# Where four tiles' statistics stand in VectorE's queue: an FNet and MLP layer on one Trainium2 core

## The chip, the core and the metric

The kernel runs on one core of a Trainium2 chip. Five engines work side by side, each through its own queue in order: TensorE (PE, matrix products into PSUM), VectorE (DVE), ScalarE (ACT), GpSimd (POOL) and SyncE (SP, which issues the DMAs). They wait for each other through semaphores. The metric is the device time of one execution in microseconds (us), smaller is better.

## The reference, cut to what matters

```python
xn = _layernorm(x, axis=-1)                       # x: (1, 2048, 576), no weights
# A: FNet mixing, the real part of a 2-D Fourier transform by matrices
a = einsum("bsd,ed->bse", xn, dft_hid_re); b = einsum("bsd,ed->bse", xn, dft_hid_im)
y = einsum("ts,bse->bte", dft_seq_re, a) - einsum("ts,bse->bte", dft_seq_im, b)
# B: MLP, 576 -> 4608 -> 576
h = maximum(einsum("bsd,df->bsf", xn, w1), 0)
out = x + y + einsum("bsf,fd->bsd", h, w2)
```

Every row of x (a token) is normalised by its own mean and variance before anything else can use it.

## The kernel before, in words

The 2048 rows are 16 tiles of 128 (tiles 0 to 15), in four groups of four. The hidden width of 4608 is cut into nine blocks of 512. All operands of products are split into two float16 parts, high and low, so each product is three matmuls; the second MLP product and the sequence transform use seven products in place of eight (Strassen in Winograd's form, `PRODUCTS`, L263).

A tile's way to TensorE has these steps. `stats` (L175) takes, for a list of tiles, two `bn_stats` of each (L182, VectorE), an aggregate of each (L185), one square root for all (L192, ScalarE), and six short VectorE steps (L193 to L204) that give the factors and shifts. `normalize` (L219) writes the normalised rows in float32 on VectorE (L224) and in float16 on ScalarE (L225). `remainder` (L227) takes the low parts, for most tiles on GpSimd (L229, L232). `transposes` (L236) turns nine pieces on TensorE (L240) into a PSUM tile `pt` and copies them to `xT` on ScalarE (L245, L248). A staging buffer of pool `dpool` (four buffers) carries a tile from `normalize` to `transposes`.

The MLP then runs over steps (block b, group g). `mlp1` (L291) makes one 128 x 512 piece of the hidden layer in 14 matmuls (L286); a block has four pieces. `mlp1_out` (L296) takes two pieces, a pair, out of PSUM: ReLU and splitting (L303, L306 and L313 on ScalarE; L307 to L311 on VectorE) and a last VectorE difference (L314), which is remembered as `order["lo"]`. `mlp2` (L318) is one of the seven second products, 12 matmuls (L328), and an accumulation into the rows on VectorE (L334). Step n computes the first product of its own group and the second product of the step before it, interleaved.

Ahead of that loop the first block's first two groups are written out by hand: `tile_by` makes the first product tile by tile in pieces of 128 columns, `max_w1`, `power_w1` and `split_w1` scale and split w1, and `prepare_w2` (L426) does so for w2: sums on ScalarE (L375), a power of two found with two small matmuls (L140, L148), and splits on ScalarE (L164) and VectorE (L165, with L405 to L408 between them). Of group 1's first product only the first pair (two pieces, in a PSUM tile `pq` of pool `ps2`) is made by hand; the other two pieces are made at step n = 1. `ps2` has two buffers, which `pq`, the `pt` tiles and the second products share.

While b is 0, each step also prepares the next group: at n = 1 tiles 8 to 11, at n = 2 tiles 12 to 15. That is the call `weave(stats(...))` at L627 and, between the pieces, `normalize`, `remainder` and `transposes` (L636 to L638).

The order of each engine's queue isn't the order of the source. The framework records all instructions with their dependencies and places them by its own costs. `tc.issue_after(ins)` adds one rule: the instructions recorded inside it, on the engine of `ins`, stand behind `ins` in that queue. It adds no semaphore. At n = 1, `order["lo"]` is the difference L314 of group 1's first pair; at n = 2, that of its second pair.

After the MLP come the hidden transform (`dft1`, L678) and the sequence transform (L779), which take no part in the change.

Of the kernel before, what the change touches and what calls it, by code (L numbers as in the profile page):

```python
# [41 lines left out]
def kernel(  # L42
# [127 lines left out]
    means, factors, shifts, order = {}, {}, {}, {}  # L170
# [4 lines left out]
    def stats(ts):  # L175

        n = len(ts)
        mv = small.tile([P, n, 2], F32, tag=f"mv{n}", name=f"mv{ts[0]}")
        sts = [small.tile([P, 2, 6], F32, tag="st", name=f"st{t}", bufs=4) for t in ts]
        for t, st in zip(ts, sts):  # L180
            for j in range(2):
                nc.vector.bn_stats(st[:, j, :], acc[t][:, j * EH : (j + 1) * EH])  # L182
                yield
        for i, st in enumerate(sts):
            nc.vector.bn_aggr(mv[:, i], st.rearrange("p a b -> p (a b)"))  # L185
            yield
        r0, u, r, sh = (
            small.tile([P, n], F32, tag=f"{a}{n}", name=f"{a}_{ts[0]}") for a in ("r0", "u", "r", "sh")
        )
        m, v = mv[:, :, 0], mv[:, :, 1]  # L190
        stt = nc.vector.scalar_tensor_tensor
        nc.scalar.activation(u, v, AF.Sqrt, bias=eps)  # L192
        nc.vector.reciprocal(r0, u)  # L193
        yield

        stt(u, v, EPS, r0, ALU.add, ALU.mult)
        yield
        nc.vector.tensor_tensor(u, u, r0, ALU.mult)
        yield
        nc.vector.tensor_scalar(u, u, -0.5 * SX, 1.5 * SX, ALU.mult, ALU.add)  # L200
        yield
        nc.vector.tensor_tensor(r, u, r0, ALU.mult)
        yield
        stt(sh, m, -1.0, r, ALU.mult, ALU.mult)  # L204
        for i, t in enumerate(ts):
            means[t], factors[t], shifts[t] = mv[:, i, 0:1], r[:, i : i + 1], sh[:, i : i + 1]

    def weave(steps, *others):

        others = list(others)  # L210
        for _ in steps:
            if others:
                others.pop(0)()
        for f in others:
            f()
# [3 lines left out]
    def normalize(t, eng=nc.vector):  # L219
        stage = dpool.tile([P, 5 * EH], F32, tag="d", name=f"xn{t}")  # L220
        xn = xns[t] = stage[:, :D]

        xs = xss[t] = stage[:, D : 2 * D].bitcast(F16)
        eng.tensor_scalar(xn, acc[t], means[t], factors[t], ALU.subtract, ALU.mult)  # L224
        nc.scalar.activation(xs[:, :D], acc[t], AF.Identity, bias=shifts[t], scale=factors[t])  # L225

    def remainder(t, eng):  # L227
        xn, xs = xns[t], xss[t]
        eng.tensor_tensor(  # L229
            xs[:, D : D + REM], xn[:, KM * P :], xs[:, KM * P : D], ALU.subtract  # L230
        )
        eng.tensor_tensor(  # L232
            xs[:, D + REM :], xn[:, : KM * P], xs[:, : KM * P], ALU.subtract
        )

    def transposes(t):  # L236
        xs = xss[t]
        pt = ps2.tile([P, 2, 1024], F16, tag="ps2", name=f"pt{t}")
        for k in range(NKX):
            nc.tensor.transpose(  # L240
                pt[:, k // 8, (k % 8) * P : (k % 8 + 1) * P], xs[:, k * P : (k + 1) * P], ident
            )
        g, c = divmod(t, TG)
        dst = xT[g][:, :, c * P : (c + 1) * P]
        nc.scalar.activation(  # L245
            dst[:, :8, :], pt[:, 0, :].rearrange("p (k t) -> p k t", t=P), AF.Copy
        )
        nc.scalar.activation(dst[:, 8, :], pt[:, 1, :P], AF.Copy)  # L248
# [42 lines left out]
    def mlp1(b, g, i):  # L291
        ps = ps1.tile([P, G], F32, tag="ps1", name=f"p1_{b}_{g}_{i}")
        mlp1_group(b, g, i, slice(0, G), ps)
        return ps

    def mlp1_out(b, g, i, pa, pb):  # L296

        h = hs[b, g, i] = mlp.tile([P, 2, 7, GH], F16, tag="h", name=f"h{b}_{g}_{i}", bufs=4)
        st = mlp.tile([P, 5, GH], F32, tag="stage", name=f"s{b}_{g}_{i}")
        stt = nc.vector.scalar_tensor_tensor  # L300
        a11, a21, a12, a22 = pa[:, :GH], pa[:, GH:], pb[:, :GH], pb[:, GH:]
        r21, s1, s2, s3, s4 = (st[:, n] for n in range(5))
        nc.scalar.activation(r21, a21, AF.Relu)  # L303
        for q, src in ((slice(A11, A11 + 1), a11), (slice(A12, A22 + 1), pb)):
            hi, lo = (h[:, n, q].rearrange("p a b -> p (a b)") for n in range(2))
            nc.scalar.activation(hi, src, AF.Relu)  # L306
            stt(lo, src, 0.0, hi, ALU.max, ALU.subtract)  # L307
        stt(s3, a11, 0.0, r21, ALU.max, ALU.subtract)
        stt(s1, a22, 0.0, r21, ALU.max, ALU.add)
        stt(s2, a22, 0.0, s3, ALU.max, ALU.subtract)  # L310
        stt(s4, a12, 0.0, s2, ALU.max, ALU.subtract)  # L311
        hi, lo = (h[:, n, S1 : S4 + 1] for n in range(2))
        order["s"] = nc.scalar.activation(hi, st[:, 1:], AF.Copy).ins  # L313
        order["lo"] = nc.vector.tensor_tensor(lo, st[:, 1:], hi, ALU.subtract).ins  # L314
# [121 lines left out]
    def prepare_block(b):  # L436

        wait = [lambda: None] * 2
        (m0, s0), (m1, s1) = prepare_w1(b, 0), prepare_w1(b, 1)
        return (  # L440
            [lambda: (load_w1(b, 0), load_w1(b, 1))] + wait
            + m0 + m1 + s0 + [lambda: load_w2(b, 0)] + s1 + [lambda: load_w2(b, 1)]
            + wait + prepare_w2(b)
        )
# [96 lines left out]
    def work():  # L541
        if todo:
            todo.pop(0)()
# [5 lines left out]
    def load_d(j):  # L549
        load_raw(("d", j), dft[:, :, j * EH : (j + 1) * EH], [P, KT, EH])  # L550

    def power_d(j):
        if j == 0:
            sc["d"], pw["d"], mx["d"] = cell("sd", 4), cell("pd", 4), cell("md", 4)
        m = slice(j, j + 1)
        magnitude(mx["d"][:, m], raws["d", j])
        power(sc["d"][:, m], pw["d"][:, m], mx["d"][:, m])
# [5 lines left out]
    def split_d(j):  # L563
        split(dsp[j][:, 0], dsp[j][:, 1], raws["d", j], sc["d"][:, j : j + 1])
# [47 lines left out]
    for n in range(1, len(steps)):  # L612
        b, g = steps[n]
        pb, pg = steps[n - 1]
        if g == 0 and b:
            if b + 1 < NB:
                todo += prepare_block(b + 1)
            else:
                todo += [lambda: (load_d(0), load_d(1)), lambda: None, new_d, lambda: None]
                for j in range(4):  # L620
                    todo += [lambda j=j: power_d(j), lambda j=j: split_d(j)]
                    if j < 2:
                        todo += [lambda j=j: load_d(j + 2), lambda: None]
                todo += [scales_d]
        if b == 0 and g + 1 < NG:
            with tc.issue_after(order["lo"]):
                weave(stats([(g + 1) * TG + i for i in range(TG)]))  # L627
        ps = []
        for i in range(NF):
            if n > 1 or i > 1:  # L630
                ps.append(mlp1(b, g, i))
                if i % 2:
                    mlp1_out(b, g, i // 2, *ps[-2:])
            if b == 0 and g + 1 < NG:
                t = (g + 1) * TG + i
                normalize(t)  # L636
                remainder(t, nc.gpsimd)
                transposes(t)  # L638
            if n == 2 and i == 2:
                todo += prepare_block(1)  # L640
            for _ in range(1 if b else 3):
                work()
            for q in range(2 * i, min(2 * i + 2, 7)):
                mlp2(pb, pg, q)
            for _ in range(1 if b else 3):
                work()
            if n > 3 and i % 2 and passes:
                passes.pop(0)()
# [196 lines left out]
```

## Time and profile before

| what | value |
|---|---|
| median of 3 runs | 1309.46 us (1308.74 to 2731.43) |
| profiled execution | 1310.21 us |
| its span, first to last instruction | 1308.4 us |
| TensorE busy | 1273.3 us, 97% |
| VectorE busy | 973.5 us, 74% |
| ScalarE busy | 532.5 us, 41% |
| GpSimd busy | 34.6 us, 3% |
| mean granted TensorE clock | 0.991 |

How rows are read: in a timeline, the start and the length in us, engine, line, operation, tile written <- tiles read, shapes, the count of merged instructions, and in brackets the idle time ahead of them with what ended it. In the table by windows the columns are the window, its length, busy time (and instructions) of PE, PEld (weight loads), DVE, ACT and POOL, then the granted TensorE clock, the busy share of the DMA engines and GB/s. In groups by line: busy us, mean ns of one, idle us ahead and what ended it. Matmul ends are modelled, and lengths of merged rows overlap the next row a little.

### The profile page before, as it was taken

The page shows a single profiled execution, that of the slowest core. Times are in us where ns is not written, and L with a number is a line of the kernel's source. Part 1 is how long each engine was busy: PE and PEld are TensorE (multiplying, and loading weights), DVE is VectorE, ACT ScalarE, POOL GpSimd, SP SyncE. Part 2 cuts the span into 40 slices and gives each one's busy share as a digit, 9 for nine tenths or more (in the row PEclk, how much of TensorE's full clock was granted, in tenths as well). Part 3 has the DMA queues.
Part 4 walks back from the last instruction along what each step waited for, and adds up shares of the span by engine and source line. Part 5 has one row for each costly group of instructions (what it writes and reads, how often), then busy time and mean ns, then how long its engine had stood idle before and what let it go on. Part 6 is the DMA issues. An engine that isn't in the chain of part 4 may idle for free.

```text
span 1308.4 us, 21689 instructions
## 1 busy us (share of the span) xinstructions
PE 1273.3 (97%) x9080; PEld 872.4 (67%) x9080; DVE 973.5 (74%) x1671; ACT 532.5 (41%) x794; POOL 34.6 (3%) x60
## 2 busy tenths in 40 slices
PE   7589999999999999999999999999999999999998
PEld 6365666666666666666666656677777777777777
DVE  7857978577586696785875885568677887878785
ACT  5644444244253443443443432234443333343332
POOL 3030000000000000000000000000000000000000
PEclk8899999999999999999999999999999999999999
DMA  6101213123122131131221232240014344343420
GB/s 238 41 1 37 74 56 111 61 73 102 49 89 85 49 106 68 49 117 56 74 87 48 94 94 85 89 150 17 1 52 171 122 135 154 97 151 117 145 83 19
DMA packets 38002, 112.75 MB, mean 86 GB/s; under 512 B 3984, under 2 KB 10640, under 8 KB 37904
## 3 DMA queue, kind: packets, MB, share of 16 engines
q1 hardware_dynamic: 37904, 111.36, 25.7%
q8 instruction: 71, 1.16, 0.4%
q14 instruction: 27, 0.22, 0.1%
HBM read 101.91 MB, written 9.44 MB: 85 GB/s over the span
## 4 chain that ended last, share of the span: by engine, by line
PE 88%; DVE 6%; DMA 2%; ACT 2%; issue 1%; POOL 0%; SPq 0%; POOLq 0%; DVEq 0%; ACTq 0%
PE p L286 29%; PE p L328 26%; PE p L779 24%; PE pd L678 8%; DVE acc L334 1%; DVE w2s L165 1%; DMA raw_d<-in_dft_dram 1%; ACT xT L245 1%; DMA c<-in_cim_dram 1%; DVE h L307 0%; DMA acc<-in_x_dram 0%; PE pt L240 0%; DVE st L182 0%; DVE cs L165 0%; DVE c_md L98 0%
## 5 line engine op out<-in xcount | busy, mean ns | idle before, releaser
L286 PE MATMUL p<-xT,w1s 128*128 128x512 f16 (+1 forms) x2268 | 462.7, 357 | 4.0 <-ACT xT L245 3.9
L328 PE MATMUL p<-w2s,h 128*128 128x288 f16 x3024 | 396.9, 287 | 3.5 <-DVE acc L334 2.3
L328 PEld LDWEIGHTS <-h 128*128 128x128 f16 x3024 | 296.2, 98 | 105.3 <-issue 4.3
L286 PEld LDWEIGHTS <-w1s 128*128 128x128 f16 x2268 | 210.2, 99 | 206.6 <-issue 5.0
L779 PE MATMUL p<-R,cs 128*128 128x288 f16 x2688 | 329.6, 286 | 1.0 <-DVE o L785 1.0
L779 PEld LDWEIGHTS <-cs 128*128 128x128 f16 x2688 | 263.0, 98 | 67.4 <-issue 1.2
L334 DVE SCALAR_TENSOR_TENSOR acc<-p,c_ub,acc 128x576 f32<-128x576 f32 x252 | 203.4, 810 | 22.6 <-PE p L328 22.1
L164 ACT ACTIVATE cs<-c,sc_c 128x1024 f16<-128x1024 f32 x112 | 128.5, 1148 | 202.9 <-PE p L779 146.9
L307 DVE SCALAR_TENSOR_TENSOR h<-p,h 128x256 f16<-128x256 f32 (+1 forms) x144 | 79.6, 554 | 146.7 <-ACT h L306 146.6
L165 DVE SCALAR_TENSOR_TENSOR cs<-c,sc_c,cs 128x1024 f16<-128x1024 f32 x112 | 143.6, 1282 | 49.0 <-ACT cs L164 48.8
L306 ACT ACTIVATE h<-p 128x512 f16<-128x512 f32 (+1 forms) x144 | 69.7, 486 | 226.4 <-PE p L286 224.1
L313 ACT ACTIVATE h<-s 128x1024 f16<-128x1024 f32 x72 | 76.1, 1057 | 172.1 <-DVE s L311 172.0
L678 PE MATMUL pd<-dsp,xT 128*128 128x288 f16 x896 | 109.9, 286 | 0.9 <-DVE acc L334 0.9
L314 DVE TENSOR_TENSOR h<-s,h 128x1024 f16<-128x1024 f32 x72 | 87.9, 1221 | 29.0 <-ACT h L313 29.0
L678 PEld LDWEIGHTS <-xT 128*128 128x128 f16 x896 | 87.7, 98 | 23.2 <-issue 1.1
L785 DVE SCALAR_TENSOR_TENSOR o<-p,us_c,o 128x288 f32<-128x288 f32 x112 | 57.4, 513 | 20.1 <-PE p L779 20.1
L605 ACT ACTIVATE f<-f 128x1024 f32<-128x1024 f32 x64 | 66.6, 1041 | 3.6 <-DMA f<-in_cre_dram 3.6
L164 ACT ACTIVATE w2s<-raw_w,c_sw 128x576 f16<-128x576 f32 (+1 forms) x54 | 44.0, 849 | 24.6 <-DVE c_sw L397 19.7
L165 DVE SCALAR_TENSOR_TENSOR w2s<-raw_w,c_sw,w2s 128x576 f16<-128x576 f32 (+1 forms) x54 | 46.5, 910 | 7.6 <-ACT w2s L164 7.6
L303 ACT ACTIVATE s<-p 128x256 f32<-128x256 f32 x72 | 26.7, 371 | 23.5 <-PE p L286 23.5
L696 ACT ACTIVATE R<-pd,c_rho 128x288 f16<-128x288 f32 x48 | 23.9, 500 | 22.0 <-DVE T L690 12.2
L240 PE MATMUL pt<-ident,xn 128*128 128x128 f16 x144 | 12.1, 227 | 20.2 <-ACT xn L225 16.0
(96 smaller groups left out, 637.7 us busy)
## 6 DMA issues: line engine op xcount, KB each, us to landing
f<-in_cre_dram SPq DMA_DIRECT2D x32, 512.0 KB, 3.5
f<-in_cim_dram SPq DMA_DIRECT2D x32, 512.0 KB, 3.5
c<-in_cre_dram SPq DMA_DIRECT2D x32, 512.0 KB, 3.9
c<-in_cim_dram SPq DMA_DIRECT2D x32, 512.0 KB, 4.6
raw_w<-in_w_dram SPq DMA_DIRECT2D x17, 640.0 KB, 4.0
raw_w<-in_w_dram SPq DMA_DIRECT2D x18, 576.0 KB, 3.9
acc<-in_x_dram SPq DMA_DIRECT2D x16, 288.0 KB, 6.7
spill<-acc SPq DMA_DIRECT2D x16, 288.0 KB, 2.5
```

What stands on the lines that cost most here:

```text
L164: nc.scalar.activation(hi, src, AF.Copy, scale=s)
L165: nc.vector.scalar_tensor_tensor(lo, src, s, hi, ALU.mult, ALU.subtract)
L286: nc.tensor.matmul(ps[:, cols], w1s[b, i // 2][:, hl, i % 2 * KT + k], xT[g][:, kx, cols], start=(n == 0), stop=(n == len(WK) - 1),)
L306: nc.scalar.activation(hi, src, AF.Relu)
L307: stt(lo, src, 0.0, hi, ALU.max, ALU.subtract)
L313: order["s"] = nc.scalar.activation(hi, st[:, 1:], AF.Copy).ins
L314: order["lo"] = nc.vector.tensor_tensor(lo, st[:, 1:], hi, ALU.subtract).ins
L328: nc.tensor.matmul(ps[:, c], h[:, x, qa, c * P : (c + 1) * P], w[:, y, qb], start=first and i == 0 and j == 0, stop=i == NQ - 1 and j == 2 ...
L334: nc.vector.scalar_tensor_tensor(o, ps, us[b], o, ALU.mult, ALU.add)
L605: nc.scalar.activation(f, f, AF.Abs, scale=2.0**-10, accum_out=sums_c[:, n, q : q + 1])
L678: nc.tensor.matmul(ps[j], xT[g][:, kx, c * P : (c + 1) * P], dsp[j][:, hl, k], start=(n == 0), stop=(n == len(XK) - 1),)
L779: nc.tensor.matmul(ps, w[:, a, k], r[:, c, rq], start=first and k == 0 and j == 0, stop=k == HK - 1 and j == 2, skip_group_check=not first,)
```

## The change

```diff
@@ -623,7 +623,7 @@
         if b == 0 and g + 1 < NG:
-            with tc.issue_after(order["lo"]):
+            with tc.issue_after(order["lo"]) if n > 1 else nullcontext():
                 weave(stats([(g + 1) * TG + i for i in range(TG)]))
```

At n = 1 the rule is gone; at n = 2 it stays. The number of instructions, their operands and sizes are the same. What moves, in the built program:

- VectorE: the eight `bn_stats` of tiles 8 to 11 stand among the short steps of tiles 4 to 7's statistics (seven of them ahead of the normalisation of tiles 4 to 7); their aggregates, their short steps and the normalisation of tile 8 follow, ahead of the first pair's L307 of group 0. The normalisations of tiles 9, 10 and 11 stand inside the work on group 0's pairs, ahead of the w2 split. Of the seven accumulations L334 of group 0, the first now stands ahead of the last difference of group 1's first pair, and the others stand behind it and among the work on the second pair; six stand ahead of the statistics of tiles 12 to 15, the seventh among them. Before, seven of the eight `bn_stats` of tiles 12 to 15 stood ahead of all of them.
- ScalarE: the copies of tile 3 come ahead of all four normalisations of tiles 4 to 7 (before, between the second and the third). The normalisations of tiles 8, 9 and 10 stand ahead of tile 7's copies; tile 8's copies and tile 11's normalisation stand between the first and the second part of the w2 split.
- TensorE: tile 8's transposes stand straight behind tile 7's pieces of the first product (128 columns each); then 10 matmuls of the third piece of group 1, product 0 (A11 B11) of group 0, 18 matmuls of the third and fourth piece, product 1 (A12 B21), and products 2 to 6 with the transposes of tiles 9, 10 and 11 between them; then the first piece of group 2 and the transposes of tile 12. Before, the third and fourth pieces were mixed into tile 7's, tile 8's transposes came behind them, and tile 12's transposes stood ahead of group 2's first piece. Behind the transposes of tile 12 the order is the same to the end.
- GpSimd and SyncE: the same order.

## The prediction

> **What bounds the kernel now.** I read the page's engine shares and slices first, then the waits of the early stage, then the timelines of the five engines there.
>
> ```profile
> span 1308.4 us, 21689 instructions
> PE 1273.3 (97%) x9080; PEld 872.4 (67%) x9080; DVE 973.5 (74%) x1671; ACT 532.5 (41%) x794; POOL 34.6 (3%) x60
> ...
> PE   7589999999999999999999999999999999999998
> ```
>
> TensorE is busy 97% of the span, so time can come only from where it isn't: the early slices of 32.7 us (digits 7, 5 and 8). Finer windows show where the holes lie.
>
> ```profile
> 36.00:40.00 4.00, 3.44 (x58) 3.10 (x56) 2.24 (x5) 3.88 (x8) 0.00 (x0) 1.00 0.00 0
> 40.00:44.00 4.00, 2.78 (x43) 2.37 (x41) 2.90 (x14) 1.98 (x3) 0.00 (x0) 1.00 0.00 0
> ...
> 52.00:56.00 4.00, 0.00 (x0) 0.00 (x0) 4.00 (x10) 1.51 (x2) 0.00 (x0) 0.86 0.55 164
> ...
> 60.00:64.00 4.00, 0.00 (x0) 0.00 (x0) 3.86 (x19) 1.84 (x3) 0.00 (x0) 0.50 0.00 0
> ...
> 70.00:72.00 2.00, 2.00 (x11) 1.24 (x10) 1.42 (x5) 0.00 (x0) 1.14 (x2) 0.52 0.00 0
> 72.00:74.00 2.00, 2.00 (x21) 1.59 (x20) 0.95 (x3) 0.24 (x1) 0.00 (x0) 1.00 0.02 4
> ```
>
> From 52 to 64 TensorE does nothing. The granted clock holds at full through windows with holes (36 to 44), falls to 0.50 about 4 us after TensorE stops, and is back at 72. The waits between 20 and 112 us name the reason:
>
> ```profile
> PE pt L240 <- ACT xn L225: 13.4, 1, 13.4
> ```
>
> and TensorE's timeline places it:
>
> ```profile
> 26.89 0.67 PE L240 MATMUL pt<-ident,xn 128*128 128x128 f16 x9
> 27.39 3.29 PE L286 MATMUL p<-xT,w1s 128*128 128x128 f16 x56
> ...
> 36.86 0.66 PE L240 MATMUL pt<-ident,xn 128*128 128x128 f16 x9 [0.49 <-ACT xT L248]
> ...
> 43.10 7.83 PE L286 MATMUL p<-xT,w1s 128*128 128x128 f16 x56 [1.00 <-ACT xT L245]
> 64.33 0.61 PE L240 MATMUL pt<-ident,xn 128*128 128x128 f16 x4 [13.40 <-ACT xn L225]
> ...
> 67.46 6.28 PE L328 MATMUL p<-w2s,h 128*128 128x288 f16 x32
> ...
> 75.60 5.55 PE L328 MATMUL p<-w2s,h 128*128 128x288 f16 x44 [0.79 <-ACT xT L248]
> ...
> 84.80 3.18 PE L286 MATMUL p<-xT,w1s 128*128 128x512 f16 x14 [0.61 <-ACT xT L245]
> 87.82 3.10 PE L328 MATMUL p<-w2s,h 128*128 128x288 f16 x24
> 90.76 3.18 PE L286 MATMUL p<-xT,w1s 128*128 128x512 f16 x14
> ```
>
> At 64.33 the transposes of tile 8 start after 13.40 us idle: tile 8 had no normalised rows, since its statistics stand behind a VectorE difference. From 84.80 on TensorE hardly waits.
>
> **A ledger.** Both programs issue the same TensorE work between two marks: the start of tile 7's first product (43.10; the row of x56 holds it and two 128x512 groups) and the first 24 matmuls of group 1's second product (87.82). At full clock: 128x512 costs (87.82-84.80)/14 = 0.216 us, 128x288 (90.76-87.82)/24 = 0.1225. So 7.83 for the x56, 5 transposed tiles at 0.5 (26.89 to 27.39), 84 matmuls of 0.1225 = 10.3, the last group 3.02: 23.65 us. Before takes 44.72. The 21.1 between them is idle time and the half clock (the 32 matmuls at 67.46 took 6.2 instead of 3.9), and is the most that this stage can give.
>
> **The change, step by step.** In the built program all of it lies ahead of 90 us; past the transposes of tile 12 TensorE's order is unchanged, GpSimd's and SyncE's are unchanged throughout, and no DMA is added or moved.
>
> ```profile
> 23.32 0.41 DVE L185 BATCH_NORM_AGGREGATE mv<-st 128x2 f32<-128x12 f32 x4
> ...
> 26.16 2.09 DVE L224 TENSOR_SCALAR xn<-acc,mv,r 128x576 f32<-128x576 f32 x4
> 32.99 0.42 DVE L307 SCALAR_TENSOR_TENSOR h<-p,h 128x256 f16<-128x256 f32 x1 [4.75 <-ACT h L306]
> ...
> 45.17 2.14 DVE L165 SCALAR_TENSOR_TENSOR w2s<-raw_w,c_sw,w2s 128x864 f16<-128x864 f32 x2
> ...
> 54.62 0.81 DVE L165 SCALAR_TENSOR_TENSOR w2s<-raw_w,c_sw,w2s 128x576 f16<-128x576 f32 x1
> ...
> 57.41 2.97 DVE L182 BATCH_NORM_STATS2 st<-acc 128x6 f32<-128x288 f32 x8
> ...
> 99.41 1.53 DVE L98 TENSOR_REDUCE c_mf<-raw_w 128x1 f32<-128x640 f32 x2
> ```
>
> *Statistics.* Eight at 0.37 (2.97/8), four aggregates at 0.1, six short steps at 0.2: some 4.6 us, out of 57.41 to 62.9 and into the slots from 23.7 on, where VectorE sat idle 4.75 us ahead of 32.99. Seven stand ahead of the normalisation of tiles 4 to 7, but partly in the gaps of its chain: I make that start 26.74, +0.6. x has landed by then:
>
> ```profile
> L80 SPq DMA_DIRECT2D acc<-in_x_dram x16: 392/432/838, 0.7 to 16.1; - x16
> ...
> DMA to landing us min/median/max: 2.9/6.7/8.0
> ```
>
> The last of 16 loads is issued at 16.1 and the slowest takes 8.0; tile 11 is four issues of 0.43 earlier, so at most 22.4, ahead of 23.7.
>
> *ScalarE.* All four normalisations of tiles 4 to 7 now stand behind tile 3's copy, and three of tiles 8 to 10 ahead of tile 7's.
>
> ```profile
> 26.60 1.62 ACT L225 ACTIVATE xn<-acc,sh,r 128x576 f16<-128x576 f32 x2
> ...
> 31.22 1.02 ACT L245 ACTIVATE xT<-pt 128x1024 f16<-128x1024 f16 x1 [0.40 <-PE pt L240]
> ...
> 36.50 0.32 ACT L248 ACTIVATE xT<-pt 128x128 f16<-128x128 f16 x1
> ...
> 42.02 1.02 ACT L245 ACTIVATE xT<-pt 128x1024 f16<-128x1024 f16 x1 [2.15 <-PE pt L240]
> ```
>
> Tile 3's transposes end at 27.55, its copies at 28.8; four normalisations at 0.76 (half of 1.62 less the overlap) end at 31.8, the square root of tiles 8 to 11, taken as a third of one, at 32.05, and tile 4's copy starts there instead of at 31.22: +0.83, which was on the chain. Nothing after it up to tile 5's copy (ending 36.82, then 37.65) gives that back, so tile 6's transposes start at 37.7 instead of 36.86. The three extra normalisations (2.4 us) fall into the 2.15 idle ahead of 42.02; tile 7's copy starts at 42.85. Tile 7's product starts at **43.9, +0.8**; the w2 split goes from 45.17 to 46.15 on VectorE, +1.0. In it VectorE is never idle, so its last split ends at 56.4 (before 55.43) and the last read of the pair's PSUM tile (L311) at 55.7, one split of 0.72 ahead of that.
>
> *TensorE after 43.9.* 28 matmuls to 45.45; tile 8's transposes to 45.95 (ScalarE's rows for them are done at 41.4, GpSimd's remainders by 44.1 even at the worst price below, 2.7); 10 of the third group's matmuls to 48.1. Product 0 needs a PSUM slot from tile 8's copy, which stands on ScalarE behind the w2 split (to 46.8) and two short reads: 48.6, **idle 0.5**. It ends at 50.1, the 18 remaining 128x512 at 54.0. Product 1 needs the PSUM slot read by L311: 55.75, **idle 1.7**; it ends at 57.2. From there each product waits for VectorE's accumulation of an earlier one (about 0.75 us each, and L314, L307 to L311 between them):
>
> ```profile
> L334 DVE SCALAR_TENSOR_TENSOR acc<-p,c_ub,acc 128x576 f32<-128x576 f32 x8 | 6.5, 816 | 4.5 <-PE p L328 4.5
> ...
> L314 DVE TENSOR_TENSOR h<-s,h 128x1024 f16<-128x1024 f32 x4 | 4.9, 1220 | 2.5 <-ACT h L313 2.5
> ```
>
> Accumulations 0, 1, 2 end at 57.1, 59.0, 59.75 (L314, 1.15, between the first two). Product 2 runs 57.2 to 58.7; tile 9 waits for accumulation 1 (**0.35**), 9 matmuls for accumulation 2 (**0.25**) to 60.9; product 3 and 3 matmuls to 62.75; product 5 waits for accumulation 3 (63.2, **0.5**) to 64.7; 10 matmuls to 65.9, tile 10 to 66.45, 2 matmuls to 66.7; tile 11 waits for tile 10's copy (67.7, **1.05**) to 68.25; the next group waits for tile 11's (69.35, **1.2**) and runs 69.4 to 72.45.
>
> *What is late next.* Tile 12. Its statistics still follow the difference L314 and here accumulation 5 (65.85): 8 statistics and accumulation 6 to 69.6, aggregates 70.0, square root and chain 71.5, ScalarE's normalisation 72.45, then GpSimd:
>
> ```profile
> 64.35 1.31 POOL L229 TENSOR_TENSOR xn<-xn 128x64 f16<-128x64 f32 x1 [30.93 <-ACT xn L225]
> 65.63 1.37 POOL L232 TENSOR_TENSOR xn<-xn 128x512 f16<-128x512 f32 x1
> ...
> 68.34 0.30 POOL L229 TENSOR_TENSOR xn<-xn 128x64 f16<-128x64 f32 x1
> 68.60 1.15 POOL L232 TENSOR_TENSOR xn<-xn 128x512 f16<-128x512 f32 x1
> ```
>
> 1.45 for the two remainders without contention (68.34, 68.60), 2.7 at worst (64.35, 65.63): 73.9 to 75.15, and 0.25 of transposes. VectorE works through tiles 13 to 15 beside it, as it worked beside the two slow rows, so I take 75.1, near the slow end: **idle 2.1**. The Trainium skill, "GPSIMD Engine Reference", section "8. Key points", says that GpSimd shares its SBUF interfaces with VectorE, in contention with some of its instructions; the 1.31 against 0.30 us for the same 64-column step agrees; by that rule the mark would lie at the slow end, 75.4.
>
> **Sum.** The second mark: 43.9 + 23.65 + 7.65 idle = 75.2, against 87.82: **12.6 us earlier**. From there the order is the old one and TensorE never waits long, so the gain stays to the end. The profiled execution took 1310.21 (span 1308.4 and 1.8 around it): **1297.6 us**, a span of 1295.8. The median of the runs shown, 1309.46, is 0.75 lower, which I leave in the range. About 2%, 26 us, is what a measurement of this kernel tells from no change; 12.6 is under it.
>
> **Rivals.**
> *A. VectorE takes over as the bound (chance 0.20).* The wait for tile 8 is replaced by the accumulation chain: three products wait on VectorE, and every copy on ScalarE is followed by another wait of 0.8 to 1.2. My hand-overs are 0.05 us each; some forty in series, and a chain of late copies, could cost 3 to 7 more. For: VectorE is busy 4.00 of 4 in 52 to 56 and 3.86 in 60 to 64. Against: the same chain at 67 to 84 shows stops of only 0.79 and 0.61. Time 1300.5 to 1304.5.
> *B. Fewer stalls (0.10).* Tile 12's wait and half of the others vanish: gain 15 to 18, 1292 to 1295.5. The bound is 21.1.
> *C. The clock doesn't hold (0.05), the slower side.* Before, TensorE rests once for long, then runs on; after, it stops about eight times between 48 and 74. If the clock stood at 0.50 all that stretch, as at 60 to 72, its 23 us of work would take 23 longer, up to 5 of it inside waits: the mark at 93 to 98, 5 to 10 us slower, 1315.5 to 1320.5. It ends slower once over 12.6 us of work run at half clock net of waits. Against: windows with 0.56 and 1.22 us of holes kept 1.00, and my longest is 1.7 where the fall took 4. The Trainium skill, "TensorE: Matmul & The Clock Gate", section "A second HAM failure mode: psum-queue depth-cycling", describes this: short stops between groups of matmuls make the gate swing between half and full clock. No row of this trace shows it; by it the time would lie anywhere between 1297.6 and the end of this rival.
> *D. Given back later, or no effect (0.08).* The next block's w1 loads come no earlier, since they wait for the w2 split:
>
> ```profile
> 52.08 3.71 SPq L90 DMA_DIRECT2D raw_w<-in_w_dram  x2
> ```
>
> Issued at about 53 and 56.5, read first at about 87 (99.41 before): they would have to be 25 us late. An unmoved order would give 1310, but the built order has the statistics ahead of 33 us. Time 1304.5 to 1310.
>
> **How the numbers follow.** Main case 0.57 (gain 10 to 15, 1295.2 to 1300.2), A 0.20, B 0.10, C 0.05, D 0.08. The range 1293 to 1304.5 holds the main case, A and most of B, about 0.83. Faster by over 2% would need more than the 21.1 of the ledger: 0.01. Slower by over 2% needs 26 us, beyond C's price: 0.02. Within 2%: 0.97.
>
> **What would show it.** Right: no TensorE idle above 3 us between 42 and 80; tile 8's transposes near 45.5; product 1 near 55.8, released by VectorE; tile 12's transposes released by GpSimd near 75; 1.00 clock from 28 on; the first 24 matmuls of group 1's second product near 75. Wrong: a clock of 0.50 in any window past 44, a w2 split that starts past 48, or an accumulation chain whose waits sum to more than 10 us.

## The result, and the profile after

The changed kernel takes **1301.14 us** (median of 4 runs, 1300.62 to 1301.37) against 1309.22 for the kernel before in the same comparison: a ratio of **0.9939, interval 0.9919 to 0.9958**. One of the four runs of the kernel before took 2731.43 us and is left out of the ratio; the other three lie between 1308.74 and 1309.46. The kernel is faster by about 8 us: the interval excludes 1, but 0.6% is under the 2% from which a difference counts here. The time is inside the predicted range, 3.5 us above the predicted 1297.6. The profiled execution took 1300.62 us.

The page of the kernel after, its engine shares and its slices of the span:

```profile
span 1298.9 us, 21692 instructions
PE 1273.3 (98%) x9080; PEld 873.1 (67%) x9080; DVE 976.9 (75%) x1671; ACT 532.5 (41%) x794; POOL 35.2 (3%) x60
...
PE   8789999999999999999999999999999999999998
```

TensorE's busy time is that of before to the tenth; the span is 9.5 us shorter. The early slices read 8, 7 and 8 where they read 7, 5 and 8. TensorE's timeline of the kernel after shows the same stage as the one quoted in the prediction:

```profile
37.66 0.66 PE L240 MATMUL pt<-ident,xn 128*128 128x128 f16 x9 [0.83 <-ACT xT L248]
...
44.53 1.72 PE L286 MATMUL p<-xT,w1s 128*128 128x128 f16 x28 [1.00 <-ACT xT L245]
46.09 0.67 PE L240 MATMUL pt<-ident,xn 128*128 128x128 f16 x9
...
50.48 1.63 PE L328 MATMUL p<-w2s,h 128*128 128x288 f16 x12 [1.57 <-ACT xT L248]
...
58.59 4.77 PE L328 MATMUL p<-w2s,h 128*128 128x288 f16 x24 [2.60 <-DVE s L311]
...
64.27 3.10 PE L328 MATMUL p<-w2s,h 128*128 128x288 f16 x24 [0.41 <-DVE acc L334]
67.92 2.85 PE L328 MATMUL p<-w2s,h 128*128 128x288 f16 x22 [0.54 <-DVE acc L334]
...
72.65 0.66 PE L240 MATMUL pt<-ident,xn 128*128 128x128 f16 x9 [1.03 <-ACT xT L248]
74.42 3.18 PE L286 MATMUL p<-xT,w1s 128*128 128x512 f16 x14 [1.11 <-ACT xT L245]
...
79.14 0.40 PE L240 MATMUL pt<-ident,xn 128*128 128x128 f16 x4 [1.10 <-POOL xn L232]
79.38 3.10 PE L328 MATMUL p<-w2s,h 128*128 128x288 f16 x24
```

The stop of 13.40 us is gone: tile 8's transposes run at 46.09. In its place stand seven stops between 0.41 and 2.60 us. The second mark (first 24 matmuls of group 1's second product) lies at 79.38 in place of 87.82, **8.4 us earlier**; it was forecast at 75.2. The span gains 1.1 more than the mark does, nearly all of it because one late wait in this trace of the kernel before has no counterpart after (its row in TensorE's timeline); no run shows that the change removed it.

```profile
1002.16 3.10 PE L779 MATMUL p<-R,cs 128*128 128x288 f16 x24 [0.96 <-DVE o L785]
```

Three rows differ from the forecast by more than half a microsecond in their stop: 50.48 and 58.59 wait longer, 79.14 (tile 12) waits 1.0 less. One takes too long: 24 matmuls in 4.77 us where 3.10 is their length at full clock (79.38). The first two stops, which follow from a late w2 split, and the clock are what most of the experiments are about.

**The late split.** VectorE's timeline of the kernel after, the steps that lie on the way to the w2 split (L165) and to the last read of the pair's PSUM tile (L311):

```profile
32.88 1.09 DVE L200 TENSOR_SCALAR u<-u 128x4 f32<-128x4 f32 x1
34.26 1.09 DVE L204 SCALAR_TENSOR_TENSOR sh<-mv,r 128x4 f32<-128x4 f32 x1
...
42.52 1.06 DVE L151 TENSOR_SCALAR c_tw<-half 128x2 int32<-128x2 int32 x1
43.90 1.05 DVE L389 TENSOR_TENSOR c_pp<-c_pw,c_pw 128x2 f32<-128x2 f32 x1
46.01 0.56 DVE L397 TENSOR_SCALAR c_sw<-c_pw,c_inv 128x2 f32<-128x2 f32 x1
48.18 2.14 DVE L165 SCALAR_TENSOR_TENSOR w2s<-raw_w,c_sw,w2s 128x864 f16<-128x864 f32 x2
...
53.52 2.37 DVE L165 SCALAR_TENSOR_TENSOR w2s<-raw_w,c_sw,w2s 128x576 f16<-128x576 f32 x2
...
58.13 0.41 DVE L311 SCALAR_TENSOR_TENSOR s<-p,s 128x256 f32<-128x256 f32 x1
```

Of these steps of two or four elements per partition, four take over a microsecond. In the kernel before, the three at the split have these lengths:

```profile
41.42 0.15 DVE L151 TENSOR_SCALAR c_tw<-half 128x2 int32<-128x2 int32 x1
...
41.89 0.14 DVE L389 TENSOR_TENSOR c_pp<-c_pw,c_pw 128x2 f32<-128x2 f32 x1
...
42.70 0.23 DVE L397 TENSOR_SCALAR c_sw<-c_pw,c_inv 128x2 f32<-128x2 f32 x1
```

GpSimd's timeline of the kernel after shows what runs beside each of the long ones, a remainder of 512 columns (L232) or the 64 columns ahead of it (L229):

```profile
32.78 1.16 POOL L232 TENSOR_TENSOR xn<-xn 128x512 f16<-128x512 f32 x1
...
34.16 1.16 POOL L232 TENSOR_TENSOR xn<-xn 128x512 f16<-128x512 f32 x1
...
42.40 1.16 POOL L232 TENSOR_TENSOR xn<-xn 128x512 f16<-128x512 f32 x1
...
43.78 1.16 POOL L232 TENSOR_TENSOR xn<-xn 128x512 f16<-128x512 f32 x1
...
45.16 1.38 POOL L232 TENSOR_TENSOR xn<-xn 128x512 f16<-128x512 f32 x1
51.26 2.17 POOL L229 TENSOR_TENSOR xn<-xn 128x64 f16<-128x64 f32 x1 [4.72 <-ACT xn L225]
53.39 1.15 POOL L232 TENSOR_TENSOR xn<-xn 128x512 f16<-128x512 f32 x1
```

Read the ends: L200 ends at 33.97, the remainder beside it at 33.94; L204 at 35.35 and 35.32; L151 at 43.58 and 43.56; L389 at 44.95 and 44.94; L397 at 46.57 and 46.54. Each of these VectorE steps starts while a remainder runs and ends with it. The reverse shows at 51.26: 64 columns that take 0.30 us elsewhere take 2.17 while VectorE goes through L406 to L408, and the split behind them takes 2.37 in place of 1.54. Not every VectorE step is held. Within the same remainders L310 and L311, which read PSUM, L393 and L399 (one element wide) and the reduction L391 keep their usual 0.41 and 0.14; the normalisation L224 at 44.88 takes 0.64 where 0.57 is usual.

In its first 100 us the kernel before had one such held short step. GpSimd's timeline of before:

```profile
24.28 1.15 POOL L232 TENSOR_TENSOR xn<-xn 128x512 f16<-128x512 f32 x1
```

and VectorE's beside it:

```profile
24.30 1.15 DVE L196 SCALAR_TENSOR_TENSOR u<-mv,r 128x4 f32<-128x4 f32 x1
```

The changed order puts the remainders of tiles 8 to 10 beside the chain that ends in the w2 split. The Trainium skill, "GPSIMD Engine Reference", section "8. Key points", states that GpSimd shares its SBUF interfaces with VectorE, in contention with some of its instructions; the rows agree, and add the size: the whole rest of the other engine's instruction.

**The clock.** Past 25 us TensorE's clock fell once. The table by windows of the kernel after, in windows chosen so that they end where the clock changes (window, length, busy time of PE, PEld, DVE, ACT, POOL, then the granted clock):

```profile
48.86:52.27 3.41, 1.84 (x15) 1.36 (x14) 3.41 (x8) 3.14 (x7) 1.01 (x1) 1.00 0.00 0
...
55.69:59.10 3.41, 0.81 (x7) 0.43 (x6) 3.41 (x8) 1.12 (x2) 0.00 (x0) 1.00 0.58 188
59.10:62.51 3.41, 3.41 (x17) 2.18 (x15) 2.84 (x4) 0.53 (x1) 0.00 (x0) 0.50 0.59 191
```

Half clock from 59.10 to 62.51 costs 4.77 - 3.10 = 1.67 us. Why it fell there is settled only by the last runs below.

### The profile page after: what moved, and what is told of

The parts are those of the page before. It is cut to its first block, busy times and chain, and to the rows that moved or that the text cites. A ratio compares the mean times of both kernels' runs of the same rounds, so it can differ in the third digit from the quotient of the medians.

```text
span 1298.9 us, 21692 instructions
## 1 busy us (share of the span) xinstructions
PE 1273.3 (98%) x9080; PEld 873.1 (67%) x9080; DVE 976.9 (75%) x1671; ACT 532.5 (41%) x794; POOL 35.2 (3%) x60
## 3 DMA queue, kind: packets, MB, share of 16 engines
q8 instruction: 71, 1.16, 0.4%
## 4 chain that ended last, share of the span: by engine, by line
PE 88%; DVE 7%; DMA 2%; ACT 1%; issue 1%; POOL 0%; SPq 0%; POOLq 0%; ACTq 0%; DVEq 0%
PE p L286 29%; PE p L328 25%; PE p L779 25%; PE pd L678 8%; DVE acc L334 1%; DMA raw_d<-in_dft_dram 1%; DVE w2s L165 1%; DVE st L182 1%; DVE h L307 0%; DMA acc<-in_x_dram 0%; DVE c_md L98 0%; DVE w1s L165 0%; DVE h L314 0%; DVE xn L224 0%; DMA raw_w<-in_w_dram 0%
## 5 line engine op out<-in xcount | busy, mean ns | idle before, releaser
L328 PE MATMUL p<-w2s,h 128*128 128x288 f16 x3024 | 396.5, 287 | 8.0 <-DVE acc L334 3.4
L328 PEld LDWEIGHTS <-h 128*128 128x128 f16 x3024 | 295.9, 98 | 110.2 <-issue 9.5
L334 DVE SCALAR_TENSOR_TENSOR acc<-p,c_ub,acc 128x576 f32<-128x576 f32 x252 | 203.5, 810 | 22.4 <-PE p L328 21.8
L307 DVE SCALAR_TENSOR_TENSOR h<-p,h 128x256 f16<-128x256 f32 (+1 forms) x144 | 79.6, 554 | 135.8 <-ACT h L306 135.6
L165 DVE SCALAR_TENSOR_TENSOR cs<-c,sc_c,cs 128x1024 f16<-128x1024 f32 x112 | 143.6, 1282 | 49.0 <-ACT cs L164 42.0
L306 ACT ACTIVATE h<-p 128x256 f16<-128x256 f32 (+1 forms) x144 | 69.8, 485 | 224.7 <-PE p L286 222.5
L164 ACT ACTIVATE w2s<-raw_w,c_sw 128x576 f16<-128x576 f32 (+1 forms) x54 | 43.9, 849 | 24.7 <-DVE c_sw L397 19.7
L165 DVE SCALAR_TENSOR_TENSOR w2s<-raw_w,c_sw,w2s 128x576 f16<-128x576 f32 (+1 forms) x54 | 47.3, 926 | 7.6 <-ACT w2s L164 7.6
L165 DVE SCALAR_TENSOR_TENSOR w1s<-raw_w,c_sw,w1s 128x640 f16<-128x640 f32 x36 | 30.9, 877 | 0.2 <-ACT w1s L164 0.2
```

Of the source, the lines that this page charges most:

```text
L164: nc.scalar.activation(hi, src, AF.Copy, scale=s)
L165: nc.vector.scalar_tensor_tensor(lo, src, s, hi, ALU.mult, ALU.subtract)
L328: nc.tensor.matmul(ps[:, c], h[:, x, qa, c * P : (c + 1) * P], w[:, y, qb], start=first and i == 0 and j == 0, stop=i == NQ - 1 and j == 2 ...
L334: nc.vector.scalar_tensor_tensor(o, ps, us[b], o, ALU.mult, ALU.add)
```

## The experiments

To compare kernels whose traces start a little differently, I use one interval: from the start of tile 7's first product to the *second* row of 24 matmuls L328 of group 1 (94.28 before, 85.84 after), which holds the same TensorE work in all of them. It repeats well: three traces of one kernel (late_b, late_c, late_d) give 39.25, 39.25 and 39.26. Times and spans repeat less well (the ten runs of half lie between 1304.15 and 1308.47), so a difference of 1 or 2 us between two spans, each of one trace, says little; the interval says more. Each ratio is to the runs of the kernel before in the same comparison.

| kernel | interval, us | clock fell in it | span, us | median, us | ratio to before |
|---|---|---|---|---|---|
| before | 51.18 | yes | 1308.4 | 1309.22 | 1 |
| after | 41.31 | yes | 1298.9 | 1301.14 | 0.9939 [0.9919, 0.9958] |
| half | 47.89 | yes | 1304.4 | 1306.25 | 0.9981 [0.9972, 0.9991] |
| quarters | 41.29 | yes | 1297.8 | 1299.92 | 0.9929 [0.9914, 0.9943] |
| late | 40.91 | yes | 1298.2 | 1299.29 | 0.9924 [0.9907, 0.9940] |
| free2 | 39.62 | yes | 1297.1 | 1299.32 | 0.9924 [0.9909, 0.9939] |
| vec | 37.67 | no | 1295.9 | 1297.16 | 0.9906 [0.9891, 0.9921] |
| latefree2 | 39.30 | yes | 1297.2 | 1297.88 | 0.9912 [0.9896, 0.9929] |
| vecfree2 | 35.91 | no | 1291.9 | 1294.90 | 0.9893 [0.9878, 0.9908] |
| vecall | 35.92 | no | 1293.6 | 1294.49 | 0.9891 [0.9876, 0.9906] |
| late_b, late_c, late_d | 39.25, 39.25, 39.26 | no | 1297.2, 1295.7, 1296.1 | one run each | - |
| after_b | 39.80 | no | 1296.5 | one run | - |

Each edit is shown against the kernel after.

**half: is the gain the shortening of tile 8's chain?** Only the eight `bn_stats` of tiles 8 to 11 are freed; their aggregates, short steps and all that follows stay behind the difference, and TensorE's order is that of before.

```diff
-            with tc.issue_after(order["lo"]) if n > 1 else nullcontext():
-                weave(stats([(g + 1) * TG + i for i in range(TG)]))
+            steps_s = stats([...]); [next(steps_s) for _ in range(2 * TG * (n == 1))]
+            with tc.issue_after(order["lo"]): weave(steps_s)
```

> Only the eight bn_stats of tiles 8 to 11 are freed; their aggregates, small steps and normalisation stay behind the difference as in the kernel before. TensorE's order is that of the kernel before. If the gain is the length of the work taken off tile 8's chain, tile 8's transposes start 2 to 3 us ahead of the 64.33 of before, the clock still falls in a hole of 10 us or more, and the span falls by 1 to 3 us (1305.5 to 1307.5). If freeing the statistics on VectorE alone carried the gain, the span would fall by 6 us or more. If the early delay of ScalarE (+1.3 us there) eats it, the span stays within 0.7 us of 1308.4.

TensorE's timeline of half:

```profile
62.17 0.61 PE L240 MATMUL pt<-ident,xn 128*128 128x128 f16 x4 [10.51 <-ACT xn L225]
```

The stop shrinks from 13.40 to 10.51 us, by 2.9, about the 2.97 of eight statistics, and the interval by 3.3. So the stop follows the length of tile 8's chain behind the difference, and taking work out of that chain shortens the stage about one for one. The span of 1304.4 lies 1.1 under the expected band; by the medians of its own comparison the gain is 2.2 (1308.45 to 1306.25), inside the expected 1 to 3. That the rest of the change's gain comes from taking out the rest of the chain fits this, but is not separated: the full change also moves TensorE's and ScalarE's orders.

**quarters: does the length of a remainder set the hold?** The 512 columns of L232 are cut into four instructions of 128 for tiles 4 to 11, all on GpSimd as before; every queue's order stays.

```diff
-        eng.tensor_tensor(
-            xs[:, D + REM :], xn[:, : KM * P], xs[:, : KM * P], ALU.subtract
-        )
+        w = P if 4 <= t < 12 else KM * P
+        for p in range(0, KM * P, w):
+            eng.tensor_tensor(xs[:, D + REM + p :][:, :w], xn[:, p : p + w], xs[:, p : p + w], ALU.subtract)
```

> The 512-column remainder of tiles 4 to 11 on GpSimd is cut into four pieces of 128 columns; the order of all other work is that of the changed kernel. Theory H (VectorE's small steps are held until GpSimd's running instruction ends): L200, L204, L151, L389 and L397, 0.56 to 1.09 us in the changed kernel, fall to 0.45 or less, the w2 split on VectorE starts at 46.2 to 46.8 instead of 48.18, and the span falls by 1 to 2 us. Rival I (VectorE waits for its own instructions, GpSimd has no part in it): those five steps keep 0.6 to 1.1 us at the same places, and the span doesn't move.

VectorE's timeline of quarters:

```profile
41.81 0.34 DVE L151 TENSOR_SCALAR c_tw<-half 128x2 int32<-128x2 int32 x1
...
42.47 0.14 DVE L389 TENSOR_TENSOR c_pp<-c_pw,c_pw 128x2 f32<-128x2 f32 x1
...
43.72 0.47 DVE L397 TENSOR_SCALAR c_sw<-c_pw,c_inv 128x2 f32<-128x2 f32 x1
...
48.61 1.28 DVE L405 TENSOR_TENSOR raw_w<-raw_w 128x288 f32<-128x288 f32 x2
```

The five steps fall to 0.14 to 0.47 us (L200 and L204 to 0.36 and 0.35), where 0.45 or less was expected; a piece takes 0.40 (1.58 for four). The split starts at 46.33 in place of 48.18; 0.70 of that is the earlier first mark of this trace (43.83 in place of 44.53). The hold goes with the length of the other engine's instruction, as expected, and rival I is out. The span is 1.1 shorter, as expected in size, but the interval doesn't move: the gain didn't reach TensorE in this stage, which I had not expected: the shorter pieces let VectorE slip between them, so GpSimd is now the one held and its work stretches into the split. GpSimd's timeline of quarters:

```profile
46.53 3.64 POOL L234 TENSOR_TENSOR xn<-xn 128x128 f16<-128x128 f32 x4
```

and TensorE's:

```profile
57.86 4.77 PE L328 MATMUL p<-w2s,h 128*128 128x288 f16 x24 [3.98 <-DVE s L311]
```

L405 to L408 take 1.15 to 1.28 a pair in place of 0.82, the two engines delay each other until 53.1, and product 1 waits 3.98. The interval is unchanged (41.29): the same contention, spread differently.

**late: take the remainders away from the split's chain.** The normalisations of tiles 9 to 11 are ordered behind the first part of the w2 split on VectorE and ScalarE, so the remainders come behind them too. The edit therefore moves the normalisations (L224, 0.57 each on VectorE) off the split's chain together with the remainders, and can't tell the two apart.

```diff
-                normalize(t)
+                with queue_behind(*order["w2", 0, 1, 0]) if n == 1 and i else nullcontext(): normalize(t)
```

> The normalisations of tiles 9, 10 and 11 stand behind the first part of the w2 split on VectorE and on ScalarE; the rest is the changed kernel. If they and the GpSimd remainders that follow them delay the split (theory H with the queue), it starts at 45.5 to 46.5 instead of 48.18, product 1 starts at 56 to 57 instead of 58.59, and the span falls by 1 to 3 us. If the split was late for the four normalisations of tiles 4 to 7 alone, it stays at 47 to 48 and the span within 0.5 us.

The split starts at 46.59, L389 is back at 0.14 and L397 at 0.23 (L151 keeps 0.73, beside tile 8's remainder), and product 1 starts at 56.18 after 1.60 us. Tile 9 then pays for it. TensorE's timeline of late:

```profile
60.46 0.23 PE L240 MATMUL pt<-ident,xn 128*128 128x128 f16 x1 [0.58 <-POOL xn L229]
61.57 0.52 PE L240 MATMUL pt<-ident,xn 128*128 128x128 f16 x4 [0.88 <-POOL xn L232]
```

and the clock fell a little later than in after. The split starts 0.1 later than the expected 45.5 to 46.5. The profiled span is 0.7 shorter, less than expected, the median 1.9 and the interval 0.4. In this trace the split's delay went back into tile 9's wait and the clock.

**vec: no GpSimd beside the split at all.** The remainders of tiles 8 to 10 run on VectorE (0.21 and 0.67 each); tile 11's stays on GpSimd.

```diff
-                remainder(t, nc.gpsimd)
+                remainder(t, nc.vector if 7 < t < 11 else nc.gpsimd)
```

> The remainders of tiles 8, 9 and 10 are made on VectorE instead of GpSimd. Theory H: L151, L389 and L397 fall from 1.06, 1.05 and 0.56 to under 0.25 us, but VectorE gets 2.7 us of remainders, so that the split starts within 0.7 us of 48.18 and the span within 1 us of the changed kernel. Rival I: the three steps stay long, the split starts at 50.5 or later and the span rises by 2 us or more.

TensorE's timeline of vec:

```profile
56.96 3.10 PE L328 MATMUL p<-w2s,h 128*128 128x288 f16 x24 [1.60 <-DVE s L311]
60.28 0.66 PE L240 MATMUL pt<-ident,xn 128*128 128x128 f16 x9 [0.21 <-DVE acc L334]
```

L151, L389 and L397 take 0.15, 0.14 and 0.21, the second part of the split 1.54, product 1 waits 1.60, and the clock stays at 1.00. The split starts at 47.37, 0.8 ahead of 48.18 where at most 0.7 was expected, although VectorE has 1.8 us of remainders ahead of it. I had put the span within 1 us of after, and it is 3.0 shorter: I had priced the work that VectorE takes over and not the second hold (2.37 to 1.54) nor the clock. Against after_b, which has no fall either, the interval is 2.1 shorter (39.80 to 37.67): that is what moving the remainders is worth, the holds taken away less the 2.6 us of work that VectorE takes over (three times 0.21 and 0.67).

**free2: tile 12.** The rule is removed for tiles 12 to 15 as well.

```diff
-            with tc.issue_after(order["lo"]) if n > 1 else nullcontext():
+            with nullcontext():
```

> The statistics of tiles 12 to 15 are freed as well. If tile 12's late chain is worth what its wait shows (1.10 idle and some 0.35 of stretched transposes), the span falls by 1 to 1.5 us. If the eight further bn_stats (3 us) in front of group 0's first pair push the w2 split back, it starts past 49.5 and the span rises by 0 to 2 us.

Tile 12's wait for GpSimd is gone, the second mark comes at 77.73 (-1.65), the interval is 1.7 shorter; the split (48.22, where 49.5 was the sign of the other outcome) and the clock's fall are those of after. The span falls by 1.8, a little over the expected 1 to 1.5. So tile 12 cost 1.65 us in after.

**The combinations.** vecfree2 joins vec and free2, latefree2 joins late and free2, and vecall is free2 with the remainders of tiles 8 to 15 all on VectorE.

> The remainders of tiles 8, 9 and 10 on VectorE, and the statistics of tiles 12 to 15 freed too. If the two gains add (3.0 and 1.8 us of span, of which tile 12's waits in the first are 1.2 us), the span is 1294 to 1295 and no window from 44 to 80 us shows a clock under 1.00. If they don't add, 1295.5 to 1297.

> The normalisations of tiles 9 to 11 behind the w2 split, and the statistics of tiles 12 to 15 freed. Tile 12's wait of 1.10 us goes, tile 9's waits for GpSimd (0.58 and 0.88) and the clock's fall stay: span 1296.5 to 1297.5.

> All remainders of tiles 8 to 15 on VectorE, statistics of tiles 12 to 15 freed. Theory H: no GpSimd instruction past 36 us, no held VectorE step past it, the clock at 1.00; but VectorE gets 0.9 us more for each of five further tiles on the chain of accumulations: span 1293.5 to 1296.5. If VectorE is the bound there, 1297 or more.

TensorE's timeline of vecfree2:

```profile
70.18 3.18 PE L286 MATMUL p<-xT,w1s 128*128 128x512 f16 x14 [1.47 <-ACT xT L245]
73.20 0.67 PE L240 MATMUL pt<-ident,xn 128*128 128x128 f16 x9
```

Tile 12's transposes follow without a wait. The two gains add: 41.31 - 35.91 = 5.4 us of interval, of which 1.5 is the absent fall (after against after_b); vec alone gave 3.6 and free2 1.7. The span of vecfree2, 1291.9, lies under the expected 1294 to 1295. vecall has the same interval and, with 1293.6, the expected span, so VectorE isn't the bound there; both are some 1.1% under the kernel before and 0.5% under after, and they can't be told apart. latefree2 met its expectation, and its clock fell from 63.0 to 66.4.

**late_b, late_c, late_d, after_b: what makes the clock fall?** By now after and free2 had fallen with a hole of 2.60 us, quarters with 3.98, late with 1.60, 0.21, 0.58 and 0.88, and vec had held with 1.60, 0.21, 0.66 and 0.31, which no length of a single hole orders. What orders them is a grid. In each of the ten traces every change of the clock lies a whole number of 3.413 us from the rise near 24 us: in before that rise is at 24.14, the fall at 54.86 (9.000 of them) and the next rise at 71.92 (14.000); in after 24.97, 59.10 (10.000) and 62.51 (11.000). The texts below call it the first rise, but each trace has an earlier one: in before the clock rises at 7.07 and falls at 17.31, 5.000 and 2.000 windows ahead of 24.14, on the same grid. Four more traces of unchanged kernels test what follows from that, with no edit.

> The kernel late once more, unchanged, for the clock alone. Theory G: the granted clock changes only at the ends of windows of 3.413 us that run on from the first rise (near 24 to 26 us), and falls where TensorE was busy for less than about 0.52 of the window (in ten traces 0.51 and less fell, 0.54 and more did not). In late such a window has to end between 61.6 and 62.7 us; where it ends elsewhere the first fall must be absent, products 2 and 3 take 3.10 in place of 4.69 us and the second mark comes 1.6 earlier, near 77.3. Rival L: the holes' own lengths decide; they are the same here, so the clock falls again at 61.7 whatever the grid.

> As for late_b: by theory G fall or no fall follows from where the windows of 3.413 us lie, counted from this trace's own first rise; by rival L the clock falls near 61.7 in every trace of this kernel.

> As for late_b: by theory G fall or no fall follows from where the windows of 3.413 us lie, counted from this trace's own first rise; by rival L the clock falls near 61.7 in every trace of this kernel.

> The changed kernel once more, unchanged, for the clock alone. Theory G: its hole of 2.60 us brings a fall if a window of 3.413 us, counted from this trace's first rise, ends between 57.7 and 60.4 us (in the time of the first trace), and none otherwise. Rival L: the clock falls again, about 3.1 us behind TensorE's stop at 56.

None of the four fell past 25 us, and by the grid none should have: moved into late's time, the windows of late_b end at 61.16 and 64.58, those of late_c at 60.39 and 63.80 and those of late_d at 60.59 and 64.01, none of them between 61.6 and 62.7; moved into after's, those of after_b end at 57.09 and 60.51, not between 57.7 and 60.4 (the second by only 0.1). The four ran on another chip than late. That chip's clock can fall too: it fell at the start of all four traces (late_b at 16.45). The windows of after_b, on the grid of its rise at 22.03:

```profile
52.75:56.16 3.41, 2.30 (x11) 0.96 (x10) 3.41 (x6) 2.31 (x6) 0.85 (x1) 1.00 0.07 12
56.16:59.58 3.42, 1.92 (x16) 1.46 (x16) 3.42 (x7) 1.06 (x1) 0.00 (x0) 1.00 0.63 192
```

The hole is the same 2.60 us, but a border between two windows cuts it at 56.16, and neither window is idle by more than half (busy 0.67 and 0.56). In after the window's border lay at 55.69, and one window held all of the hole (0.81 of 3.41, 0.24). The same holds for late, here with the window that ended in its fall:

```profile
58.29:61.70 3.41, 1.73 (x17) 1.09 (x15) 3.41 (x5) 0.44 (x1) 1.42 (x2) 1.00 0.43 169
```

and for late_b, its least busy window:

```profile
54.00:57.41 3.41, 1.81 (x15) 1.18 (x13) 3.41 (x8) 2.18 (x3) 0.00 (x0) 1.00 0.56 192
```

Busy 0.51 and a fall, 0.53 and none. From 25 us on to the last products, over all fourteen traces, the clock fell behind each full-clock window that was busy for 0.51 or less of its 3.41 us, and behind none that was busy for 0.53 or more. The first 25 us don't keep to this border. Two windows from there, the first of after, the second of half:

```profile
7.90:11.31 3.41, 1.86 (x17) 1.21 (x17) 3.41 (x13) 3.02 (x4) 0.00 (x0) 1.00 1.02 398
```

```profile
10.89:14.31 3.42, 1.72 (x28) 1.55 (x27) 3.42 (x10) 1.46 (x4) 0.00 (x0) 1.00 0.73 259
```

Behind the first, busy for 0.54, the clock fell (so it did in after_b and latefree2); behind the second, busy for 0.50, it held (so it did in late, free2, vec, vecall and late_c). So the border is not one number by this measure, in which the ends of matmuls are modelled: between a trace's first rise and its last products, every full-clock window of 0.41 or less brought a fall, none over 0.55 did, and between these two both happened. The rise goes the same way in the kernel before:

```profile
65.09:68.50 3.41, 1.73 (x10) 1.20 (x11) 3.41 (x9) 1.50 (x2) 3.41 (x5) 0.50 0.00 0
68.50:71.92 3.42, 3.42 (x16) 2.17 (x15) 1.35 (x6) 1.15 (x3) 2.64 (x4) 0.50 0.00 0
```

0.51 busy left it at half, a full window brought it back at 71.92. In the first 25 us a window of 0.80 sufficed (after_b, 18.62 to 22.03) and one of 0.74 did not (after, 18.14 to 21.55). Theory L, the holes' own lengths, is out: equal holes fell in one trace and not in the other. The Trainium skill, "TensorE: Matmul & The Clock Gate", section "What's actually happening", gives the window as 3413 ns, free-running, not reset when a kernel starts; all fourteen traces agree. It lets the clock drop after an idle window; here a window that was half busy was enough, and the measurement decides.

So part of what the other runs showed is where the grid fell. The fall costs 1.66 us in late (40.91 against 39.25) and 1.5 in after (41.31 against 39.80). Sliding a window of 3.413 us along TensorE's busy times from 44 to 86 us in steps of 0.05, and taking 0.525 as the border, a fall follows in after_b for 2.7 us of the 3.41 that the grid can be shifted by, in late_b for 1.7, in vecfree2 for 0.7. This is an estimate that hangs on the border: with 0.545 the three are 3.2, 3.5 and 1.9. With either border vecfree2, which has the shortest stops, falls least often; shorter stops don't exclude the fall. The repeats of late also show that its gain over after is 0.55 us of interval where neither falls.

## Why the prediction was right or wrong

The total was right, inside the range, and the direction and the freed wait were right for the reasons given. The size came out short: 8.4 us at the second mark where 12.6 was forecast. The median lies outside the band of the main case (1295.2 to 1300.2) and inside the one kept for rival A, whose mechanism did not happen; that the range held it is in part luck. Step by step:

- **What bounds the kernel, and the ledger: right.** The whole change of the time lies ahead of the second mark, but for the 1.0 us at 1002. The bound of 21.1 us wasn't approached.
- **Statistics early, x landed: right, but for two short steps.** Tile 4's copy starts at 32.04 (forecast 32.05), tile 6's transposes at 37.66 (37.7). Of the short steps priced at 0.2, L200 and L204 took 1.09 each beside the remainders of tiles 4 to 7.
- **First mark: 43.9 forecast, 44.53 in the first trace, 43.58 in after_b.** The two traces of one kernel differ by more than the miss; their clocks rise at 24.97 and 22.03. So no cause of this miss is shown.
- **The w2 split "+1.0": wrong, mis-sized.** It measured +3.0 (48.18), of which 0.6 is the late first mark; in after_b it is +2.1 (47.23). The step priced the moved VectorE work and took GpSimd's queue as unchanged, which it is; it left out that the remainders of tiles 8 to 10 now run at 42 to 47 us beside the short steps ahead of the split. Three of them take 2.15 us longer together (1.06, 1.05 and 0.56 against 0.15, 0.14 and 0.23). The row at 24.30 showed such a hold before the change. I had used the contention only as a price on GpSimd, for the remainders of tiles 8 and 12, and not on VectorE.
- **Product 0, idle 0.5: 1.57. Product 1, idle 1.7: 2.60.** Both follow from the split: its ScalarE part runs to 48.8 ahead of tile 8's copy, and the second hold puts L311 at 58.13 in place of 55.7.
- **The accumulation chain: right.** Forecast 0.35 and 0.25 before tile 9's and the next matmuls, then 0.5, 1.05 and 1.2; measured 0.41, 0.54, 1.03 and 1.11; the wait ahead of tile 9 is hidden behind the slow products 1 and 2 in this trace, and is 0.21 in after_b. Rival A, VectorE as the bound, did not happen; the median lies in its band of times for other reasons.
- **Tile 12, idle 2.1: too large.** GpSimd releases it, as forecast, after 1.10, and the transposes ahead of it come some 0.35 slower; by free2 the place costs 1.65. Its two remainders took 0.60 and 1.37, between the two prices weighed.
- **Clock 1.00 from 28 us on: wrong in the first trace, right in after_b.** The step argued from "my longest is 1.7 where the fall took 4", that is from the length of a single stop. What counts is the busy share of a fixed window; the fall in before came 4 us behind the stop because the window that was idle had to end. The price was 1.67 us, one window of half clock, not the 23 us of rival C: a single busy window brought the clock back.
- **Smaller terms.** A product that waits loses about 0.16 us beside its listed idle (24 matmuls end 3.10 after their start, and the next starts 2.94 after it where nothing waits); six such places, of which the ledger's 7.83 already held one, make the 0.8 that the listed idles leave open.

The sum at the second mark: 0.63 (first mark) + 1.07 + 0.90 (products 0 and 1) + 1.67 (clock) + 0.8 (ends) - 0.65 (tile 12) - 0.26 (accumulation chain) = 4.2, the whole of 79.38 - 75.2. In after_b, without the fall, the mark lies at 76.92.

Of the signs for right, the kinds held: no idle above 3 us, product 1 released by VectorE, tile 12 by GpSimd. Their times did not: product 1 started at 58.59 (55.8 forecast), tile 12's late transposes at 79.14 and the mark at 79.38 (75 for both), and the clock fell. Two of the signs for wrong came: 0.50 in a window past 44, and a split that starts past 48. Rivals B and D did not happen: the loads of the next block bring no wait, and the gain of 8.4 at the second mark is still 8.6 at 128.39 (137.02 before).

## What to carry to other kernels

When work is moved in time, look at what then runs beside it on the *other* engine: several kinds of GpSimd and VectorE instructions that both work on SBUF took turns here, so a step of 0.15 us can last as long as the neighbour's instruction, and a chain of short steps should not lie beside long GpSimd instructions. To forecast the clock, lay a grid of 3.41 us over TensorE's timeline and take the busy share of each window at several offsets: near half busy the outcome is open, well below it the clock fell each time, and a fall that lasted one window cost 1.5 to 1.7 us here. The length of a single stop doesn't tell. A freed wait is worth at most the length of the chain that caused it, less the stops that the next tiles make of it: 13.40 us of wait became 8.4 us here.

## What the runs showed of the hardware that was not expected

- Short VectorE steps on SBUF tiles of two or four elements per partition ended only with the GpSimd instruction that was running: 0.14 to 0.17 us became 1.05 to 1.09 beside a remainder of 1.16. Steps that read PSUM, are one element wide, reduce, or take a reciprocal were not held, nor was the normalisation L224 (0.64 for 0.57). No run here shows why just these.
- The hold goes both ways: a GpSimd step of 0.30 us took 2.17 beside VectorE's two-input steps, and with remainders cut in four, four pieces took 3.64 us in place of 1.58.
- The granted clock changed only on a grid of 3.413 us, in all fourteen traces. Windows busy for 0.41 or less brought a fall, windows over 0.55 none; the border lay between 0.51 and 0.53 past 25 us, but not in the first 25. The same kernel falls in one execution and not in another (after and after_b, late and late_b), worth 1.5 to 1.7 us.
